# When the weights of a second MoE are prepared and where its input is staged: hooks replaced by slots of their own, three more staging places

## The chip, the cores and the metric

The kernel runs on one core of a Trainium2 chip. The time is device microseconds of one execution. TensorE (PE in the profile) does the matmuls, VectorE (DVE), ScalarE (ACT) and GpSimd (POOL) the elementwise work, and SyncE (SP) issues most of the DMAs. Each engine works through its own instructions in the order in which the program emits them and waits on semaphores for the others.

## The reference, cut to what matters

An attention with softmaxes over q and k gives x (2304 tokens x 512). A first mixture of experts (four experts of 1024 hidden columns, weighted by probabilities) is followed by a second layer, which the kernel calls the second MoE and which the change is about:

```
h = x @ w_in                       # 2304 x 512 @ 512 x 2048
g = where(h > 0, h, exp(min(h, 0)) - 1)
out = g @ w_out                    # 2304 x 2048 @ 2048 x 512
```

Everything is float32. A matmul is made of three in a faster format: each operand is split into a high part (a copy, on ACT) and a low part (the difference, on DVE or POOL), and the kernel adds high x high, high x low and low x high.

## The kernel before, in words

After the attention and the first expert, the work goes in 30 **steps** (s, b): s counts sets of four blocks of 128 hidden columns (s = 0 to 5 belong to the first MoE, s = 6 to 9 to the second), b = 0, 1, 2 counts thirds of the tokens. Step number i is 3 s + b, so the second MoE is steps 18 to 29. A step has 14 **products** (index `idx` 0 to 13: seven products of a Strassen-like scheme, for two halves `fp` of the hidden columns), each of six matmuls of 384 columns at line L1169. Between the products, PE does the second layer of the step before: six chunks of 12 matmuls (`chunk`, after s = 5), eight groups (`group`, after s = 6), or seven `turned_product`s after products 1, 2, 4, 6, 8, 11 and 13 (steps after s = 7, 8 and 9). The turned products take the weight parts in the order B11, T1, T2, B22, T3, B21, T4; the parts of set s are first used in the step after (s, 0), and each turned product reads the high part first and the low part in its second matmul.

After each product the loop emits the work of the other engines, in this order: the elementwise work of the product (`elu`: three ACT operations per quarter; its DVE part `rest` one or two products later; `flush` puts out the split of the results, an ACT copy at L1191 and a POOL difference at L1192), `drain`, the delayed additions of turned products (DVE, L1307), the DMA loads of the next step's input (`ring_load`, SP), the filling second-layer work, and then `tick`, which calls **hooks** up to a goal given in a table (`EARLY`, `PLAIN`, `MIXED`, `TURNED_HOOKS`); there are 24 hooks a step. Work for later steps is tied to hook numbers by `at2`.

Three kinds of such work matter here:

- `w1_steps(s, p)` prepares four weight tiles for half p of set s: four high parts `hi(0..3)` on ACT, low parts `lo(0..3)` on DVE or POOL, and two pairs of sums in place (`sums1`, `sums2`).
- `w2_fast` prepares the seven second-layer parts: `w2_sum` (DVE, L814) makes T1, T3, T2 and T4 in place; `w2_parts` makes the high part on ACT (L805) and the low part on POOL (L806).
- `turn_steps(b, c)` stages the input of the second MoE. For each third b of the tokens and each column c = 0, 1, 2, two accumulator tiles are transposed on PE (L957), copied back by ACT (L958), and seven pieces are formed with POOL differences (L992), copied to a place (`emit`, ACT or POOL), their low parts formed at L986, and stored to DRAM (L981). A place can be written again when its store has landed. There are six places, of which four are names that stand for tiles of their own (`y`, `qh`, `ql`, `extra`); in the second MoE other tiles replace these. `ring_load` reads the stored pieces back as the input of steps 18 to 20.

The transposes of column c need the accumulations of chunks c and c + 3 of the step before (DVE, L1258, after the chunks at idx 1, 3, 5, 8, 10 and 12). In the kernel before, column 2's begin at hook 22 of the same step, after product 13.

`w_load` reads raw weights from DRAM into two buffers that the two layers share, on SP's queue for s over 6. `CONV` times the conversion of float64 weights on DVE, which uses the tile `gt`; `gt` has four slots of 384 columns.

Of the kernel before, what the change touches and what calls it, by code (L numbers as in the profile page):

```python
# [21 lines left out]
def tile_attention_moe_moe(  # L22
# [13 lines left out]
    nc = tc.nc  # L36
# [676 lines left out]
    w1r, w2r, w1s, w2s = {}, {}, {}, {}  # L713

# [23 lines left out]
    def w1_steps(s, p):  # L738

        r, t = [], []  # L740

        def begin():
            r.append(w1r.pop((s, p)).rearrange("p j (d f) -> p j d f", d=KD))
            for _ in range(4):
                t.append(wp.tile([P, 2, KD, P], F32R, tag="w1", name="w1s"))
            if s % 2:
                t[0], t[2] = t[2], t[0]
            hi(0)

# [13 lines left out]

        tt = nc.vector.tensor_tensor

        def lo(k):
            eng = nc.gpsimd if k == 3 else nc.vector
            eng.tensor_tensor(out=dst(k, 1), in0=src(k), in1=dst(k, 0).bitcast(F32), op=ALU.subtract)

        def sums1():  # L770
            f1, f2 = r[0][:, 0], r[0][:, 1]
            tt = (nc.gpsimd if s == S_MOE else nc.vector).tensor_tensor
            tt(out=f1[:, :2], in0=f1[:, :2], in1=f2[:, :2], op=ALU.subtract)
            tt(out=f2[:, :2], in0=f2[:, :2], in1=f2[:, 2:], op=ALU.add)

        def sums2():
            f1, f2 = r[0][:, 0], r[0][:, 1]
            tt = (nc.vector if s > S_MOE and p else nc.gpsimd).tensor_tensor
            tt(out=f2[:, 2:], in0=f2[:, 2:], in1=f1[:, :2], op=ALU.subtract)
            tt(out=f1[:, 2:], in0=f1[:, 2:], in1=f2[:, 2:], op=ALU.subtract)  # L780

        if s > S_MOE:
            at_ = (-2, 0, 1, 4, 6, 6.5, 8, 9, 10, 11) if p else (-6, -4, -3, 1, 3, 4, 6, 8, 9, 11)
            return dict(zip(at_, (
                begin, lambda: lo(0), sums1, lambda: hi(1), lambda: lo(1), sums2,
                lambda: hi(2), lambda: lo(2), lambda: hi(3), lambda: lo(3),
            )))
# [12 lines left out]

    def w2_parts(s, op):

        src = w2_raw(s, W2_HOME.get(op, op))
        t = wp.tile([P, 2, 2, HALF_M], F32R, tag="w2", name="w2g")
        nc.scalar.activation(out=t[:, 0], in_=src, func=AF.Copy)  # L805
        nc.gpsimd.tensor_tensor(out=t[:, 1], in0=src, in1=t[:, 0].bitcast(F32), op=ALU.subtract)  # L806
        w2g[s, op] = t
# [8 lines left out]
    def w2_fast(i, s, d):  # L816

        for k, fn, op in (
            (8, w2_parts, "B11"), (14, w2_parts, "B22"), (16, w2_sum, "T1"), (17, w2_sum, "T3"), (18, w2_parts, "T1"),
            (20, w2_sum, "T2"), (21, w2_parts, "B21"), (24, w2_parts, "T2"), (30, w2_sum, "T4"), (31, w2_parts, "T3"),  # L820
            (35, w2_parts, "T4"),
        ) if s > S_MOE else (
# [5 lines left out]
            put(k - d, lambda fn=fn, op=op: fn(s, op))  # L828

# [46 lines left out]
    CONV += [(later, end1 + t, 1, True) for t in (11, 25, 39)]  # L876
# [7 lines left out]
    for i, (s, b) in enumerate(STEPS):  # L884
# [7 lines left out]
        if b == 0:  # L892

            a2, b2, c2, d2, a1, b1 = (2, 13, 25, 29, 34, 38)
            if s > 0 and (s <= S_FAST or SEVEN[s]):
                at2(i, 2, lambda s=s: w_load(s, 0, 1))
                at2(i, 13, lambda s=s: w_load(s, 1, 1))
                if SEVEN[s]:
# [7 lines left out]
            elif s > S_MOE:  # L906
                a1, b1 = (35, 40)
# [13 lines left out]
    stage = ["y", "qh", "ql", "extra", "ek"]  # L921

    def staged():
# [7 lines left out]
        if "ek" in stage:  # L931
            stage[-1:] = two(tmp, "ek")
        if now >= 0 and any(isinstance(t, str) for t in stage):
            stage[:] = two(stg, "r") + [t for t in stage if not isinstance(t, str)]
        if now >= 9 and len(stage) == 4:
# [478 lines left out]
    EARLY = {1: 4, 2: 8, 5: 12, 8: 16, 9: 20, 12: 22, 13: 24}  # L1414
    PLAIN, MIXED = ({1: 4, 3: 8, 5: 12, 8: 16, 10: 20, 12: 22, 13: 24}, {
# [13 lines left out]
    for i, (s, b) in enumerate(STEPS):  # L1429
# [11 lines left out]
        for fp in range(2):  # L1441
# [3 lines left out]
            for p in range(len(PRODUCTS)):  # L1445
# [52 lines left out]
                if i >= NB * S_MOE:  # L1498
                    drain()
# [23 lines left out]
    assert not timed2, sorted(timed2)  # L1523

# [49 lines left out]
```

## Time and profile before

| what | us |
|---|---|
| median of 3 runs | 1227.62 |
| lowest and highest | 1227.27 and 1228.93 |
| the profiled execution, its own time | 1229.85 |
| its span, first to last instruction | 1228.0 |

The profile is of one execution. It lists busy time by engine, what each engine waited for, and the clock that the throttle granted TensorE (1.00 is the full 2.4 GHz, 0.50 is 1.2 GHz). A wait for several semaphores is put down to the one that came last. An engine that is idle without being the one that others wait for costs nothing.

### The profile page before, as it was taken

What the parts mean: (1) busy time and instruction counts of PE and PEld (TensorE: products, weight loads), DVE (VectorE), ACT (ScalarE), POOL (GpSimd) and SP (SyncE); (2) the same over time, 40 slices, a digit from 0 to 9 for tenths busy, and PEclk for the clock granted to TensorE, in tenths of its full rate; (3) what the DMA queues carried; (4) which work ended last, traced back from release to release, by engine and by line L of the source; (5) the groups of instructions that cost most, each with busy time, mean ns of one, the idle gap of its engine ahead of it and who ended that gap; (6) DMA issues with size and microseconds to landing.
All of it is one profiled execution on the core that took longest, in us unless ns stands there. A gap on an engine that the chain in (4) does not pass through costs nothing.

```text
span 1228.0 us, 21080 instructions
## 1 busy us (share of the span) xinstructions
PE 1182.3 (96%) x7516; PEld 1126.5 (92%) x7516; DVE 913.1 (74%) x1523; ACT 674.7 (55%) x1431; POOL 640.2 (52%) x603
## 2 busy tenths in 40 slices
PE   8799999999999999999999999899999998898898
PEld 6688888889999999999999998788999998898898
DVE  6877887655787887787877876556557889889875
ACT  6544444236455455455455544446677776676663
POOL 4522543027468467467466453256336756756654
PEclk9999999999999999999999999889999999999999
DMA  9345666745767767667767677897965565365352
GB/s 257 113 128 161 205 217 222 265 173 215 250 226 254 261 228 250 258 234 254 254 240 253 249 244 280 283 305 257 318 245 196 195 221 181 124 228 170 148 205 103
DMA packets 157399, 272.34 MB, mean 222 GB/s; under 512 B 12784, under 2 KB 83952, under 8 KB 157296
## 3 DMA queue, kind: packets, MB, share of 16 engines
q1 hardware_dynamic: 155568, 267.87, 63.5%
q10 hardware_dynamic: 1728, 3.15, 0.7%
q8 instruction: 59, 0.97, 0.3%
q14 instruction: 44, 0.36, 0.1%
HBM read 224.83 MB, written 46.14 MB: 221 GB/s over the span
## 4 chain that ended last, share of the span: by engine, by line
PE 74%; DVE 12%; ACT 5%; DMA 4%; issue 3%; POOL 2%; SPq 0%; DVEq 0%; POOLq 0%; ACTq 0%
PE o L1387 18%; PE m L1169 14%; PE h L1169 14%; PE h L1028 7%; PE o L1028 7%; PE o L1298 6%; DVE accs L1307 2%; DMA xs<-staged 2%; DVE half L1218 1%; DMA xs<-stage 1%; PE o L1252 1%; PE o L1253 1%; PE o L1251 1%; DVE half L1219 1%; PE o L1273 1%
## 5 line engine op out<-in xcount | busy, mean ns | idle before, releaser
L1169 PE MATMUL m<-xh,w1s 128*128 128x384 f32 x840 | 250.0, 342 | 3.7 <-DVE half L1219 2.5
L1169 PE MATMUL h<-xh,w1s 128*128 128x384 f32 x840 | 246.0, 338 | 4.4 <-DVE m L1458 2.4
L1169 PEld LDWEIGHTS m<-xh,w1s 128*128 128x128 f32 x840 | 157.1, 191 | 9.6 <-DVE half L1219 4.0
L1169 PEld LDWEIGHTS h<-xh,w1s 128*128 128x128 f32 x840 | 155.7, 189 | 7.8 <-DVE m L1458 3.0
L1169 PE MATMUL m<-xl,w1s 128*128 128x384 f32 x420 | 142.5, 339 | 0.0
L1169 PE MATMUL h<-xl,w1s 128*128 128x384 f32 x420 | 141.3, 336 | 0.0
L1028 PE MATMUL o<-w2t,hpa 128*128 128x512 f32 x432 | 118.2, 401 | 0.8 <-DVE hpa L1060 0.5
L1028 PE MATMUL h<-xh,w1t 128*128 128x256 f32 (+1 forms) x512 | 113.0, 299 | 0.1
L1028 PEld LDWEIGHTS h<-xh,w1t 128*128 128x128 f32 x512 | 86.8, 193 | 5.2 <-POOL w1t L442 0.3
L1387 PE MATMUL o<-w2g,xh 128*128 128x256 f32 x540 | 90.4, 282 | 0.0
L1028 PEld LDWEIGHTS o<-w2t,hpa 128*128 128x128 f32 x432 | 75.7, 189 | 14.9 <-DVE hpa L1060 2.4
L1387 PE MATMUL o<-w2g,hpa 128*128 128x256 f32 x540 | 89.0, 282 | 0.0
L1387 PE MATMUL o<-w2g,xl 128*128 128x256 f32 x540 | 87.3, 282 | 0.0
L1409 DVE SCALAR_TENSOR_TENSOR accs<-o,pn,accs 128x256 f32<-128x256 f32 x180 | 75.7, 475 | 14.8 <-PE o L1387 14.2
L806 POOL TENSOR_TENSOR w2g<-r,w2g 128x512 fp32r<-128x512 f32 x56 | 77.9, 1398 | 15.5 <-ACT w2g L805 15.1
L1169 PEld LDWEIGHTS m<-xl,w1s 128*128 128x128 f32 x420 | 80.3, 191 | 0.5
L1169 PEld LDWEIGHTS h<-xl,w1s 128*128 128x128 f32 x420 | 79.8, 190 | 0.4
L1387 PEld LDWEIGHTS o<-w2g,xh 128*128 128x128 f32 x540 | 78.1, 190 | 0.0
L1028 PE MATMUL h<-xl,w1t 128*128 128x256 f32 (+1 forms) x256 | 77.7, 304 | 0.0
L1387 PEld LDWEIGHTS o<-w2g,hpa 128*128 128x128 f32 x540 | 76.1, 190 | 0.2
L1387 PEld LDWEIGHTS o<-w2g,xl 128*128 128x128 f32 x540 | 75.7, 190 | 0.2
L1307 DVE TENSOR_TENSOR accs<-o,accs 128x768 f32<-128x768 f32 (+1 forms) x64 | 59.5, 935 | 12.2 <-PE o L1298 12.2
(309 smaller groups left out, 3011.1 us busy)
## 6 DMA issues: line engine op xcount, KB each, us to landing
xh<-xs SPq DMA_DIRECT2D x210, 384.0 KB, 5.6
xl<-xs SPq DMA_DIRECT2D x210, 384.0 KB, 6.2
r<-in_w_dram SPq DMA_DIRECT2D x56, 256.0 KB, 4.5
xs<-stage SPq DMA_DIRECT2D x38, 256.0 KB, 5.1
xs<-xh SPq DMA_DIRECT2D x21, 384.0 KB, 3.8
xs<-xl SPq DMA_DIRECT2D x21, 384.0 KB, 4.1
r<-scratch SPq DMA_DIRECT2D x24, 256.0 KB, 3.4
x<-in_w_in_dram SPq DMA_DIRECT2D x10, 512.0 KB, 3.9
```

The costliest lines, as they stand in the source:

```text
L806: nc.gpsimd.tensor_tensor(out=t[:, 1], in0=src, in1=t[:, 0].bitcast(F32), op=ALU.subtract)
L1028: nc.tensor.matmul(out, lhsT, rhs, **kw)
L1169: nc.tensor.matmul(dst, t[:, wl, c + dl, :], x[xl_][:, dl, :], start=(n == 0 and p < 2), stop=(n == 5), skip_group_check=True,)
L1218: nc.vector.scalar_tensor_tensor(out=m, in0=m, scalar=1.0, in1=t, op0=ALU.add, op1=ALU.mult)
L1219: nc.vector.scalar_tensor_tensor(out=g, in0=h, scalar=0.0, in1=m, op0=ALU.max, op1=ALU.add)
L1251: nc.tensor.matmul(o, gh, w[:, 0, :], start=(f == 0), stop=False)
L1252: nc.tensor.matmul(o, gh, w[:, 1, :], start=False, stop=False)
L1253: nc.tensor.matmul(o, gl, w[:, 0, :], start=False, stop=(f == FS - 1))
L1298: nc.tensor.matmul(y[:, m], l, r, start=(n == 0 and k in STARTS), stop=(n == 5), skip_group_check=True)
L1307: nc.vector.tensor_tensor(out=a, in0=y[:, ms], in1=a, op=ALU.add)
L1387: nc.tensor.matmul(o, l, r, start=(first_write and m == 0 and c != 1), stop=(m == 5), skip_group_check=True)
L1409: nc.vector.scalar_tensor_tensor(out=a, in0=sums[x][:, c * HALF_M : (c + 1) * HALF_M], scalar=pr, in1=a, op0=ALU.mult, op1=ALU.add)
```

## The change

- **Staging.** Column 0 of a third starts at hook 7 (with one empty turn ahead), column 1 at hook 23 (product 13), column 2 at hook 3 of the next step. All columns go through `streams`, one entry per product and at most two streams at a time; before, only the last third did, and only from step 18. Three more places in `gt` join the list from step 17 on. Two conversions on `gt` move 3 and 6 hooks earlier, and `PLAIN` and `EARLY` reach hook 24 at product 12.
- **Slots.** For s = 7, 8 and 9 each operation of `w1_steps` and of the second-layer preparation is put at a product of its own (`put_at`; index -12 to 26, counted from product 0 of step (s, 0)) and is emitted after that product's own work and `drain`. High and low parts are emitted apart.
- **Engines.** For each of these sets, five operations go from POOL to DVE: the second pair of sums of half 0, `lo(3)` of half 0, and the low parts of T2 and B21.
- **Roles.** The four tiles of a half change roles from set to set, so that each is written when the set before has read it last.
- **Raw loads.** The next set's are tied to hooks 38 and 46, before 35 and 40.

```diff
-            eng = nc.gpsimd if k == 3 else nc.vector
+            eng = nc.gpsimd if k == 3 and (p or s <= S_MOE) else nc.vector
...
-            tt = (nc.vector if s > S_MOE and p else nc.gpsimd).tensor_tensor
+            tt = (nc.vector if s > S_MOE else nc.gpsimd).tensor_tensor
...
         if s > S_MOE:
-            at_ = (-2, 0, 1, 4, 6, 6.5, 8, 9, 10, 11) if p else (-6, -4, -3, 1, 3, 4, 6, 8, 9, 11)
-            return dict(zip(at_, (
+            i = NB * s
+            for idx, fn in zip((-5, -4, 1, -3, 2, 2, 3, 4, 4, 5) if p else (-12, -11, -11, -10, -9, -5, -4, -2, -2, 0), (
                 begin, lambda: lo(0), sums1, lambda: hi(1), lambda: lo(1), sums2,
                 lambda: hi(2), lambda: lo(2), lambda: hi(3), lambda: lo(3),
-            )))
+            )):
+                put_at(i, idx, fn)
+            return {}
...
+    def w2_slots(i, s):
+
+        for idx, fn, *a in (
+            (5, w2_hi, "B11"), (6, w2_lo, "B11"), (10, w2_sum, "T1"), (11, w2_hi, "T1"), (11, w2_sum, "T3"),
+            (12, w2_lo, "T1"), (12, w2_hi, "B22"), (13, w2_lo, "B22"), (15, w2_sum, "T2"), (16, w2_hi, "T2"),
+            (17, w2_lo, "T2", nc.vector), (18, w2_hi, "T3"), (19, w2_lo, "T3"), (23, w2_hi, "B21"),
+            (24, w2_lo, "B21", nc.vector), (24, w2_sum, "T4"), (25, w2_hi, "T4"), (26, w2_lo, "T4"),
+        ):
+            put_at(i, idx, lambda fn=fn, a=a: fn(s, *a))
...
+        if now >= -SH and not more_places:
+            y = gt.rearrange("p k n -> p (k n)").bitcast(F32R)
+            more_places.extend(y[:, k * DM : (k + 1) * DM].rearrange("p (l n) -> p l n", l=2) for k in range(3))
+            stage[:0] = more_places
...
-        for c, n0 in enumerate((8, 16, 22)):
-            fns = turn_steps(b, c)
-            if b == NB - 1:
-                at2(i, n0 - (n0 == 22), lambda f=fns: streams.append([lambda: (f[0](), f[1]()), *f[2:]]))
-                continue
-            for m, n in enumerate((0, 1, 2, 4, 5, 7, 8)):
-                if i * SH + n0 + n >= NB * S_MOE * SH:
-                    at2(i, 23, lambda f=fns[m:]: streams.append(f))
-                    break
-                at2(i, n0 + n, fns[m])
+        for c, n in enumerate((7, SH - 1, SH + 3)):
+            f = turn_steps(b, c)
+            f[:2] = [lambda f=(f[0], f[1]): (f[0](), f[1]())]
+            at2(i, n, lambda f=[lambda: None] * (c == 0) + f: streams.append(f))
...
-                if i >= NB * S_MOE:
-                    drain()
+                drain()
+                for fn in slots.pop((i, idx), ()):
+                    fn()
```

The old list of `w2_fast` for s over 6 had both parts of B11, B22, T1, B21, T2, T3 and T4 at hooks 8, 14, 18, 21, 24, 31 and 35 (the last is product 6 of step (s, 1)), and the sums T1, T3, T2 and T4 at hooks 16, 17, 20 and 30.

## Rows read from the trace of the kernel before

**Rows 1.** The page: busy time of PE, and its granted clock by slices.
```profile
PE 1182.3 (96%) x7516; PEld 1126.5 (92%) x7516; DVE 913.1 (74%) x1523; ACT 674.7 (55%) x1431; POOL 640.2 (52%) x603
PEclk9999999999999999999999999889999999999999
```
**Rows 2.** Windows, steps 16-19, 22, 24-26: length, PE, PEld, DVE, ACT, POOL, PEclk, DMA.
```profile
736.82:776.67 39.85, 34.88 (x182) 31.18 (x181) 23.52 (x40) 15.59 (x31) 12.03 (x12) 0.94 0.86 301
776.67:815.49 38.82, 35.93 (x183) 32.36 (x181) 20.59 (x34) 17.57 (x36) 15.85 (x19) 0.94 0.91 295
815.49:853.78 38.29, 36.12 (x183) 32.66 (x181) 21.84 (x34) 23.50 (x51) 19.72 (x23) 0.94 0.72 237
853.78:888.59 34.81, 33.43 (x184) 32.79 (x183) 17.34 (x29) 22.57 (x49) 16.66 (x19) 0.95 0.98 322
...
951.11:980.98 29.87, 29.63 (x170) 29.08 (x169) 26.24 (x38) 23.44 (x50) 22.00 (x20) 1.00 0.52 190
...
1010.11:1044.84 34.73, 30.89 (x170) 28.95 (x169) 33.22 (x45) 21.78 (x47) 21.72 (x19) 1.00 0.56 195
1044.84:1079.91 35.07, 31.32 (x169) 30.68 (x169) 28.27 (x40) 24.09 (x51) 22.98 (x20) 0.95 0.43 158
1079.91:1109.06 29.15, 29.15 (x170) 29.14 (x169) 24.65 (x39) 21.08 (x46) 16.35 (x17) 1.00 0.60 214
```
**Rows 3.** Waits of PE from 700 us on: total, times, longest.
```profile
PE o L957 <- DVE accs L1258: 10.0, 3, 5.0
PE o L1298 <- DVE accs L1307: 9.5, 6, 2.8
```
**Rows 4.** Timeline of PE, around 775, 853 and 1054 us.
```profile
775.08 1.30 PE L957 MATMUL o<-ident,accs 128*128 128x128 f32 x5 [4.97 <-DVE accs L1258]
...
852.93 1.09 PE L957 MATMUL o<-ident,accs 128*128 128x128 f32 x8 [2.17 <-DVE accs L1258]
...
1054.25 3.31 PE L1298 MATMUL o<-hpa,w2g 128*128 128x384 f32 x12 [2.79 <-DVE accs L1307]
```
**Rows 5.** Waits of DVE from 700 us on.
```profile
DVE stage L986 <- DMA xs<-stage: 11.0, 4, 4.3
...
DVE staged L986 <- DMA xs<-staged: 7.8, 3, 3.1
```
**Rows 6.** Timeline of DVE at the end of step 16.
```profile
773.58 0.69 DVE L986 TENSOR_TENSOR stage<-accs,stage 128x512 fp32r<-128x512 f32 x1 [3.73 <-DMA xs<-stage]
774.19 0.74 DVE L1258 SCALAR_TENSOR_TENSOR accs<-o,pn,accs 128x512 f32<-128x512 f32 x1
```
**Rows 7.** DVE's groups by line and shape in steps 24 and 25.
```profile
L1218 DVE SCALAR_TENSOR_TENSOR half<-half 128x384 f32<-128x384 f32 x8 | 8.0, 999 | 1.3 <-ACT half L1209 1.2
...
L773 DVE TENSOR_TENSOR r<-r 128x256 f32<-128x256 f32 x1 | 1.1, 1120 | 0.0
```
**Rows 8.** The same view in step 26.
```profile
L773 DVE TENSOR_TENSOR r<-r 128x256 f32<-128x256 f32 x1 | 0.4, 418 | 0.0
```
**Rows 9.** POOL's groups by line and shape in steps 24 and 25.
```profile
L806 POOL TENSOR_TENSOR w2g<-r,w2g 128x512 fp32r<-128x512 f32 x7 | 10.3, 1465 | 1.2 <-ACT w2g L805 1.2
```
**Rows 10.** Timeline of PE, ACT, POOL, DVE, products 11 to 13 of step 25.
```profile
1073.87 0.57 DVE L1469 TENSOR_TENSOR h<-h,extra 128x384 f32<-128x384 f32 x1 [0.62 <-PE h L1169]
...
1076.99 0.49 ACT L1207 ACTIVATE extra<-m 128x384 f32<-128x384 f32 x1 [0.49 <-PE m L1169]
...
1077.83 2.24 PE L1298 MATMUL o<-xh,w2g 128*128 128x384 f32 x12
...
1078.50 0.51 ACT L1191 ACTIVATE hpa<-gt 128x384 fp32r<-128x384 f32 x1
...
1079.09 1.02 POOL L1192 TENSOR_TENSOR hpa<-gt,hpa 128x384 fp32r<-128x384 f32 x1 [1.50 <-ACT hpa L1191]
```
**Rows 11.** Windows right after two of the waits of Rows 4: granted clock.
```profile
775.08:778.90 3.82, 3.82 (x15) 3.82 (x16) 1.94 (x4) 2.12 (x4) 0.00 (x0) 0.50 0.99 333
```
**Rows 12.** Timeline of SP: the first input load of step 19.
```profile
838.70 0.60 SPq L710 DMA_DIRECT2D xh<-xs  x1
```

More of the change, by code (lines that the diff above doesn't have):

```diff
@@ L713, in tile_attention_moe_moe, with put_at @@
     w1r, w2r, w1s, w2s = {}, {}, {}, {}
+    slots, roles = {}, {}
+    def put_at(i, idx, fn):
+        slots.setdefault((i + idx // 14, idx % 14), []).append(fn)
     def w_load(s, p, layer):
@@ L745, in begin @@
                 t.append(wp.tile([P, 2, KD, P], F32R, tag="w1", name="w1s"))
-            if s % 2:
+            if s > S_MOE:
+                u = roles.get(p, list(range(4)))
+                roles[p] = [u[2], u[0], u[3], u[1]]
+                t[:] = [t[k] for k in roles[p]]
+            elif s % 2:
                 t[0], t[2] = t[2], t[0]
@@ L799, in tile_attention_moe_moe, with w2_hi, w2_lo @@
     W2_HOME = {"T1": "B11", "T3": "B12", "T2": "B22", "T4": "B21"}
-    def w2_parts(s, op):
[L803 to L807, printed above, removed]
+    def w2_hi(s, op):
+        t = wp.tile([P, 2, 2, HALF_M], F32R, tag="w2", name="w2g")
+        nc.scalar.activation(out=t[:, 0], in_=w2_raw(s, W2_HOME.get(op, op)), func=AF.Copy)
+        w2g[s, op] = t
+    def w2_lo(s, op, eng=None):
+        t = w2g[s, op]
+        (eng or nc.gpsimd).tensor_tensor(
+            out=t[:, 1], in0=w2_raw(s, W2_HOME.get(op, op)), in1=t[:, 0].bitcast(F32), op=ALU.subtract
+        )
+    def w2_parts(s, op):
+        w2_hi(s, op)
+        w2_lo(s, op)
     def w2_sum(s, op):
@@ L818, in w2_fast @@
         for k, fn, op in (
[L819 to L822, printed above, removed]
             (8, w2_parts, "B11"), (13, w2_sum, "T1"), (17, w2_parts, "T1"), (18, w2_parts, "B22"), (19, w2_sum, "T3"),
@@ L875, in tile_attention_moe_moe @@
     ]
-    CONV += [(later, end1 + t, 1, True) for t in (11, 25, 39)]
+    CONV += [(later, end1 + t, 1, True) for t in (11, 22, 33)]
     end2 = NB * S_MOE * SH
@@ L897, in tile_attention_moe_moe @@
                 at2(i, 13, lambda s=s: w_load(s, 1, 1))
-                if SEVEN[s]:
+                if s > S_MOE:
+                    w2_slots(i, s)
+                elif SEVEN[s]:
                     w2_fast(i, s, 0)
@@ L906, in tile_attention_moe_moe @@
             elif s > S_MOE:
-                a1, b1 = (35, 40)
+                a1, b1 = (38, 46)
             if more and not SEVEN[s] and not SEVEN[s + 1]:
@@ L918, in tile_attention_moe_moe @@
                 at2(i, 13 + n, fn)
-    stage = ["y", "qh", "ql", "extra", "ek"]
+    stage, more_places = ["y", "qh", "ql", "extra", "ek"], []
     def staged():
@@ L932, in staged @@
             stage[-1:] = two(tmp, "ek")
+        if now >= -SH and not more_places:
+            y = gt.rearrange("p k n -> p (k n)").bitcast(F32R)
+            more_places.extend(y[:, k * DM : (k + 1) * DM].rearrange("p (l n) -> p l n", l=2) for k in range(3))
+            stage[:0] = more_places
         if now >= 0 and any(isinstance(t, str) for t in stage):
             stage[:] = two(stg, "r") + [t for t in stage if not isinstance(t, str)]
-        if now >= 9 and len(stage) == 4:
+        if now >= 9 and len(stage) == 7:
             stage[:0] = two(stg, "r")
@@ L1413, in tile_attention_moe_moe @@
     CHUNKS = (3, 0, 4, 1, 5, 2)
-    EARLY = {1: 4, 2: 8, 5: 12, 8: 16, 9: 20, 12: 22, 13: 24}
-    PLAIN, MIXED = ({1: 4, 3: 8, 5: 12, 8: 16, 10: 20, 12: 22, 13: 24}, {
+    EARLY = {1: 4, 2: 8, 5: 12, 8: 16, 9: 20, 12: 24}
+    PLAIN, MIXED = ({1: 4, 3: 8, 5: 12, 8: 16, 10: 20, 12: 24}, {
         0: 2, 1: 4, 2: 6, 3: 7, 4: 9, 5: 10, 6: 13, 7: 14, 8: 16, 9: 17, 10: 19, 11: 20, 12: 23, 13: 24,
@@ L1523, in tile_attention_moe_moe @@
     assert not timed2, sorted(timed2)
+    assert not slots and not streams, (sorted(slots), streams)
 _OUTS = [((512, 2304), "float32")]
```

## The prediction

> **What bounds the kernel now.** The page comes first: PE is busy 96% of the span, so what is to be had is only where PE is idle or slow, and the clock line shows where to look: two slices fall below 9 [rows 1]. The windows by step show the rest. Step 26 is what a second-MoE step costs undisturbed: 29.15 us, no PE idle, clock 1.00. Steps 24 and 25 have the same matmuls and take 34.73 and 35.07; together they lose 69.80 - 58.30 = 11.5 us. The set s = 9 repeats this in steps 27 and 28, so these two sets lose 23.0. Step 22, the same place in set s = 7, loses 29.87 - 29.15 = 0.7 [rows 2].
>
> The other loss is in steps 16 to 19, while the input is staged. PE idles 4.97, 2.89, 2.17 and 1.38 us there (length less PE's column), 11.4 in all. The clock's column, 0.94, 0.94, 0.94, 0.95, costs (1 - clock) x length, 2.4 + 2.3 + 2.3 + 1.7 = 8.7, of which I put 1.5 on idle time (an estimate). The loss is 11.4 + 7.2 = 18.6 us [rows 2]. Together with 23.0 and 0.7, 42.3 us are the most that could come back.
>
> What ends these waits: the two largest rows are transposes that wait for an accumulation on DVE (three times, up to 5.0), and turned products that wait for DVE's additions (six times) [rows 3]. The timeline gives single gaps; a low clock follows the large ones [rows 4], as after the first of them: 3.82 us at 0.50, the lower level of 1.2 GHz [rows 11].
>
> **Staging.** Why is DVE late at the end of step 16? Its accumulation at 774.19 stands right behind a low part that had waited 3.73 us for a store to free its place [rows 6]; such waits recur [rows 5]. Column 2's transposes follow one product after the chunk whose accumulation they need. The change moves them to product 2 of the next step: products 0, 1, 2 and one chunk later. Twelve matmuls of 384 columns take 2.08 us (from 1077.83 to the step's end at 1079.91 [rows 2, 10]), so a product takes 1.04 and a chunk, 12 of 512 columns, 2.8: 3 x 1.04 + 2.8 = 5.9 us. That is more than any of the three waits (4.97 at most), and with nine places instead of six, and stores begun before the input loads crowd the same queue, DVE should be less late as well. I take the three waits and the clock behind them as gone.
>
> Against that, two streams at once now run in products 2 to 4 of steps 17 to 19, with ACT, DVE and POOL work of two columns in one product. Step 19, which already had such an overlap before, idled 1.38 with no transposes late. I leave 1 us of new wait in each of three steps: 3.0. Bounds: 1 (only step 19's remains) and 10 (half of today's). Gain 18.6 - 3.0 = **15.6**, between 8.6 and 17.6. The moved transposes and conversions are the same instructions and cost nothing; their cover is the slack of engines that are 30 to 65% busy there [rows 2].
>
> **Weight work on DVE.** In step 24 DVE is busy 33.22 of 34.73 us, in step 26 24.65 of 29.15 [rows 2]. Part of that is lost in collisions with POOL: the same 256-column sum takes 1.120 us in step 24 and 0.418 in step 26, and the 384-column step L1218 has a mean of 0.999 [rows 7, 8]. The five operations that move are per set: two sums (0.42 each on DVE without collision), and three 512-column low parts, by L773's 0.418 for half the columns 0.7 to 0.84 each; say 0.8 + 3 x 0.7 = 2.9 us more for DVE per set. For POOL they are three of L806's 1.465 and two sums of about half, 5.9 us less [rows 9].
>
> By step, DVE without weights has about 24.65 - 2.6 = 22.0 in step 26 (two low parts, one half low part and two sums are its weights). After the change step b = 0 has 4.8 us of weight work (six low parts and sums of half 0 and 1, and the sums T1 and T3), b = 1 2.7, b = 2 4.1. That gives 26.8, 24.7 and 26.1 of 29.15, before further collisions. With POOL's weight work in b = 0 falling from six low parts to four, I add 2 us to b = 0: 28.8, nearly full. So I expect DVE to keep up, with 0.5 us of PE waits left in b = 0 and 0.5 for parts that are now made one product ahead. Bounds: 0 and today's 5.6 (step 24's loss).
>
> **A new wait: the low part of T4.** This part goes from product 6 to product 12 of step b = 1, and the turned product that reads it follows product 13. The order of emission decides: after product 12 come ACT's three operations for that product's quarter, the ACT copy and POOL difference of the quarter before (flush), and only then the slot with T4's low part, on POOL. In step 25, an undisturbed stretch, product 12 has ended by 1076.79 (the turned product's start at 1077.83 less product 13's 1.04), ACT begins the quarter at 1076.99, the copy runs at 1078.50, POOL's difference at 1079.09 until 1080.11; PE starts the turned product at 1077.83, and its second matmul would be 0.17 later (2.08 us / 12), at 1078.00 [rows 10]. T4's low part can start at 1080.11 and takes 1.465 [rows 9]: it ends at 1081.6. PE waits 3.6 us. Two more operations on DVE (low part of B21, sum of T4) now stand in front of L1469 at 1073.87 [rows 10], and by 0.7 to 1.7 us the ACT chain behind it shifts. I take 1.0: **4.6 us**, bounds 3.4 and 5.4. A wait of that length lies between those of 2.17 and 4.97, both followed by a low clock: 3.82 us at half speed cost 1.9 [rows 4, 11]. I add 2.0 (bounds 0 and 3). So 6.6 us in each of steps 22, 25 and 28. The Trainium skill (TensorE: Matmul & The Clock Gate, section "Architectural detail") states that ACT and DVE are strictly first in, first out, and GpSimd too for each of its cores; by that rule POOL cannot take T4's part ahead of the waiting difference, and rows 10 agree: POOL is idle for 1.50 us before it.
>
> What is queued behind it on POOL: the differences of the next quarters, which wait for ACT anyway until after the step's end; SP's raw load for the next set at hook 46 waits for this part too, with no input load behind it until product 7 of the next step.
>
> T1's low part has the same place in step 24, but is read after product 2 of step 25, two fills and four products later; T3's falls at product 5 and is read after product 8, with 0.5 us to spare. Both cost nothing beyond the 0.5 above.
>
> **Roles and raw loads** take away waits of ACT for tiles still being read; no wait of PE is laid to them, and I put them at nothing. Their cover is that tiles free two products before they are rewritten; without it the cost is one product, 1.0 us per set.
>
> **The sum.** Sets 8 and 9: today 11.5 each, after 6.6 + 1.0 = 7.6: gain 3.9 x 2 = 7.8. Set 7: today 0.7, after 6.6 + 0.5 = 7.1: loss 6.4. Staging: gain 15.6. Net gain 15.6 + 7.8 - 6.4 = 17.0. The profiled execution of 1229.85 (span 1228.0) goes to 1212.9; the median, 2.2 lower, 1227.6 to **1210.6**.
>
> **Rivals.**
> *The wait for T4 is not paid.* PE could reach this turned product late anyway, because DVE still holds it up, or the order on POOL could leave more room than I read. Then the three 6.6 fall away: 1210.6 - 19.8 = 1191, or 1195 with 1 us each left and the clock intact. Against it: step 25's stretch from product 9 on runs undisturbed [rows 2, 10]. Chance 0.2.
>
> *DVE stays the bound.* The collisions follow POOL's busy time, 21.7 and 23.0 us in steps 24 and 25 [rows 2]; taking 5.9 of 44.7 away leaves 87% of them. Then step 24's 5.6 stays and T4's 6.6 is added: 12.2 against 11.5, a loss of 0.7 x 2, and with 6.4 for set 7 the time is 1227.6 - 15.6 + 1.4 + 6.4 = 1220. The Trainium skill (SBUF — State Buffer, section "Who interferes with whom") has a rule for it: a VectorE instruction with two SBUF inputs and a GpSimd instruction that reads SBUF exclude each other for a whole instruction. L773 with 1.120 against 0.418 agrees [rows 7, 8]. Against it: step 26, with 16.35 of POOL, has little of it [rows 2]. Chance 0.13.
>
> *More places don't help.* DMA was busy 0.86 to 0.98 in steps 16, 17 and 19 [rows 2]; if the engines and not the places delay the stores, DVE waits as before and half the gain goes, 7.8 us: 1218. Chance 0.1.
>
> *Slower: the input lands late.* The last store of a column falls at product 7 instead of about 4, some three products and two chunks (8.7 us) later, at the very loads that read it back. The first load of step 19 was issued at 838.70, 15.1 us before the step began at 853.78 [rows 2, 12]. With 5 us to land and the waits of 2 to 4 us gone from the step's end, 6 us are left. If each load waits 12 us more for its store, steps 18, 19 and 20 wait 6 us each and lose 2 to the clock: 24, against the 17 of the forecast: 1210.6 + 24 = 1235. It decides from 5.5 us late per step. Against it: of the column's seven pieces only the last two are so late. Chance 0.07.
>
> **How the numbers follow.** The forecast has 0.5; its own range, from the bounds of the T4 wait (three times 3.4 to 8.4) and of staging, not all taken at one end, is 1203 to 1219. The range of 1195 to 1222 takes in the first rival's upper half, DVE and the places. About 0.2% is what a measurement of this kernel tells from no change: under 1225.2 faster. Faster 0.5 + 0.2 + 0.1 + most of 0.13 = 0.90; same 0.04; slower 0.06.
>
> **What would show it.** Right: no transposes among PE's waits; one gap of 3 to 5 us before the last turned product of steps 22, 25, 28, ended by POOL's low part, with a low clock after it; step 24 near 30 us and step 25 near 36; step 22 longer than before. Wrong: PE waiting for DVE's additions as before, DMA among PE's waits in steps 18 to 20, or step 22 undisturbed.

## The result: 0.8% slower, and the profile after

| | us |
|---|---|
| before, median of 4 runs (range) | 1228.28 (1227.27 to 1230.26) |
| after, median of 4 runs (range) | 1237.97 (1236.81 to 1238.73) |
| ratio, 95% interval | 1.0076, 1.0059 to 1.0094 |
| forecast | 1210.6, range 1195 to 1222 |

The kernel became slower, and the time lies outside the range. From the page of after, PE's busy time and its clock by slices; they answer to [rows 1]:

```profile
PE 1182.8 (96%) x7516; PEld 1126.6 (91%) x7516; DVE 924.3 (75%) x1537; ACT 673.0 (54%) x1430; POOL 627.0 (51%) x590
PEclk8999999999999999999999999999999899899989
```

The two 8s of before are gone; one stands in the first slice now and three near the end. The lines of the program have moved: in after, L1194 are the products, L1323 the turned products, L1332 their additions on DVE, L1217 POOL's differences of the quarters, L776 and L820 the low parts of the first and second layer's weights. In a timeline the bracket gives the idle time before a row and what ended it. The windows of after for steps 16 to 19, 22 and 24 to 26 (columns as in [rows 2]), and a stretch inside step 25:

```profile
735.69:768.97 33.28, 33.21 (x173) 29.75 (x173) 20.16 (x37) 12.77 (x26) 8.36 (x8) 1.00 0.76 267
768.97:802.95 33.98, 33.98 (x183) 30.80 (x182) 21.43 (x36) 17.26 (x37) 15.95 (x19) 1.00 1.06 354
802.95:840.03 37.08, 34.47 (x184) 30.64 (x182) 22.32 (x37) 23.39 (x50) 22.23 (x27) 1.00 0.84 275
840.03:873.25 33.22, 32.49 (x191) 32.14 (x190) 18.23 (x29) 24.59 (x53) 17.39 (x21) 1.00 0.92 314
936.81:974.50 37.69, 32.39 (x169) 30.60 (x169) 33.48 (x45) 23.66 (x50) 22.91 (x19) 0.94 0.54 189
1004.80:1040.01 35.21, 30.26 (x170) 29.02 (x170) 33.33 (x48) 23.39 (x51) 19.48 (x17) 1.00 0.57 201
1040.01:1080.51 40.50, 33.45 (x169) 32.23 (x169) 34.16 (x46) 23.56 (x50) 22.83 (x19) 0.90 0.50 176
1080.51:1110.74 30.23, 30.23 (x169) 30.22 (x169) 22.70 (x34) 19.96 (x43) 14.33 (x13) 0.96 0.43 145
...
1076.00:1082.80 6.80, 5.97 (x19) 5.98 (x20) 4.20 (x6) 0.13 (x1) 0.77 (x1) 0.50 0.66 216
```

Against [rows 2], steps 16 to 19 are 14.2 us shorter and run at full clock (step 20 gives 1.0 back). Step 22 is 7.8 longer, step 24 0.5 longer although POOL works 2.2 less in it, step 25 5.4 longer. DVE is busy 90.2 us in steps 24 to 26, before 86.1.

What PE waited for from 700 us on in after (total, times, longest), which answers to [rows 3]:

```profile
PE o L1323 <- POOL w2g L820: 12.2, 3, 4.1
PE o L1323 <- DVE accs L1332: 8.5, 6, 2.3
PE m L1194 <- DVE half L1244: 3.3, 2, 1.7
PE h L1194 <- DVE m L1483: 3.2, 2, 1.6
PE h L1194 <- ACT m L1479: 2.7, 2, 2.0
```

The transposes' row of 10.0 us is gone. In its place stands one with 12.2: the turned products that wait for T4's low part on POOL. The row of DVE's additions has hardly changed (8.5 for 9.5, six times in both), and two more rows of DVE stand under it. The single gaps in the timeline of PE, steps 24 and 25 of after, beside [rows 4]:

```profile
1007.66 0.44 PE L1194 MATMUL m<-xh,w1s 128*128 128x384 f32 x1 [1.66 <-DVE half L1244]
...
1013.79 0.81 PE L1323 MATMUL o<-hpa,w2g 128*128 128x384 f32 x3 [1.67 <-DVE accs L1332]
...
1032.59 0.44 PE L1194 MATMUL h<-xh,w1s 128*128 128x384 f32 x1 [1.62 <-DVE m L1483]
...
1047.63 2.73 PE L1323 MATMUL o<-hpa,w2g 128*128 128x384 f32 x10 [2.26 <-DVE accs L1332]
...
1076.83 1.65 PE L1323 MATMUL o<-xh,w2g 128*128 128x384 f32 x4 [4.07 <-POOL w2g L820]
```

The gap at 1076.83 is the forecast one. The clock is 0.50 for 6.8 us there (the window above), from 0.83 us before PE goes on to 5.97 after. The four before it are DVE's. The timeline of DVE and POOL in step 24 shows what makes DVE late:

```profile
1024.85 0.64 DVE L1248 TENSOR_TENSOR gt<-half,gt 128x384 f32<-128x384 f32 x1
1025.04 1.60 POOL L776 TENSOR_TENSOR w1s<-r,w1s 128x512 fp32r<-128x512 f32 x1
1025.53 1.53 DVE L1249 TENSOR_TENSOR gt<-gt 128x384 f32<-128x384 f32 x1
1026.59 1.61 POOL L820 TENSOR_TENSOR w2g<-r,w2g 128x512 fp32r<-128x512 f32 x1
1026.97 1.64 DVE L1250 TENSOR_TENSOR half<-half,gt 128x384 f32<-128x384 f32 x1
1028.16 1.32 POOL L1217 TENSOR_TENSOR hpa<-gt,hpa 128x384 fp32r<-128x384 f32 x1
1028.54 1.36 DVE L1243 SCALAR_TENSOR_TENSOR half<-half 128x384 f32<-128x384 f32 x1
```

Two low parts and a quarter's difference follow each other on POOL, and three 384-column operations of DVE take 1.53, 1.64 and 1.36 us, where 0.56 is their time with POOL out of the way (shown below). Each of the three ends 0.41 or 0.42 us after the POOL operation beside it has ended (for L1249: 1027.06 against 1026.64), as if it had to let that one pass first. The slots of their own put the two low parts beside DVE's own work.

### The profile page after: what moved, and what is told of

Read it like the earlier page. It is cut to its first block, busy times and chain, and to the rows that moved or that the text cites. A ratio compares the mean times of both kernels' runs of the same rounds, so it can differ in the third digit from the quotient of the medians.

```text
span 1236.9 us, 21090 instructions
## 1 busy us (share of the span) xinstructions
PE 1182.8 (96%) x7516; PEld 1126.6 (91%) x7516; DVE 924.3 (75%) x1537; ACT 673.0 (54%) x1430; POOL 627.0 (51%) x590
## 4 chain that ended last, share of the span: by engine, by line
PE 68%; DVE 12%; issue 6%; POOL 6%; ACT 5%; DMA 3%; SPq 0%; DVEq 0%; POOLq 0%; ACTq 0%
PE o L1412 18%; PE m L1194 13%; PE h L1194 12%; PE h L1053 7%; PE o L1053 6%; PE o L1323 3%; DMA xl<-xs 2%; DVE accs L1332 2%; POOL w2g L820 2%; PE o L1277 1%; PE o L1278 1%; PE o L1276 1%; POOL xl L1217 1%; DVE half L1244 1%; ACT half L1233 1%
## 5 line engine op out<-in xcount | busy, mean ns | idle before, releaser
L1194 PE MATMUL h<-xh,w1s 128*128 128x384 f32 x840 | 245.6, 338 | 7.3 <-DVE m L1483 3.2
L1194 PE MATMUL m<-xh,w1s 128*128 128x384 f32 x840 | 248.3, 340 | 3.9 <-DVE half L1244 3.3
L1194 PEld LDWEIGHTS h<-xh,w1s 128*128 128x128 f32 x840 | 155.6, 189 | 10.4 <-DVE m L1483 3.9
L1194 PEld LDWEIGHTS m<-xh,w1s 128*128 128x128 f32 x840 | 156.4, 190 | 8.7 <-DVE half L1244 3.9
L1194 PE MATMUL m<-xl,w1s 128*128 128x384 f32 x420 | 141.9, 338 | 0.0
L1194 PE MATMUL h<-xl,w1s 128*128 128x384 f32 x420 | 141.1, 336 | 0.0
L1053 PEld LDWEIGHTS h<-xh,w1t 128*128 128x128 f32 x512 | 86.1, 192 | 5.2 <-POOL w1t L442 0.3
L1053 PEld LDWEIGHTS o<-w2t,hpa 128*128 128x128 f32 x432 | 75.6, 189 | 14.9 <-DVE hpa L1085 2.4
L1194 PEld LDWEIGHTS m<-xl,w1s 128*128 128x128 f32 x420 | 80.2, 191 | 0.5
L1194 PEld LDWEIGHTS h<-xl,w1s 128*128 128x128 f32 x420 | 79.7, 190 | 0.3
L820 POOL TENSOR_TENSOR w2g<-r,w2g 128x512 fp32r<-128x512 f32 x50 | 71.6, 1444 | 11.0 <-ACT w2g L814 11.0
L1217 POOL TENSOR_TENSOR hpa<-gt,hpa 128x384 fp32r<-128x384 f32 x27 | 29.4, 1094 | 80.9 <-ACT hpa L1216 66.8
```

The lines of the kernel that those rows point to most:

```text
L820: (eng or nc.gpsimd).tensor_tensor(out=t[:, 1], in0=w2_raw(s, W2_HOME.get(op, op)), in1=t[:, 0].bitcast(F32), op=ALU.subtract)
L1053: nc.tensor.matmul(out, lhsT, rhs, **kw)
L1194: nc.tensor.matmul(dst, t[:, wl, c + dl, :], x[xl_][:, dl, :], start=(n == 0 and p < 2), stop=(n == 5), skip_group_check=True,)
L1217: nc.gpsimd.tensor_tensor(out=gl, in0=g, in1=gh.bitcast(F32), op=ALU.subtract)
```

## The experiments

Each time below is the median of four executions (no roles: five), and each ratio is against the kernel before, run beside it. These medians of before lie between 1225.79 and 1227.63 us, so kernels of different rounds are compared by ratio.

### Staging alone, weight work alone

*Only staging*: the weight preparation of before, the staging of after. *Only slots*: the other half.

> The staging part alone, with the weights prepared as before. Theory (the loss lies in the weight slots): steps 16 to 20 as in the changed kernel, which took 13.2 us less there than before, and steps 22, 24, 25, 27, 28 as before: 1228 - 13 = 1215. Rival (the staging part gives its gain back later, in the second MoE's own steps): above 1222.

> The slots, engines, roles and raw loads alone, with the staging as before. Theory: the sets s = 7, 8, 9 lose what they lose in the changed kernel, 9.0 + 7.0 + 6.9 = 22.9 us more than before: 1251. Rival (the two parts disturb each other): under 1243.

Measured: staging alone 1219.24 us, ratio 0.9928 (0.9909 to 0.9946); slots alone 1246.87, ratio 1.0158 (1.0143 to 1.0173). The two are worth -8.4 and +19.2 us against 1227.63 beside them; their sum, +10.9, is close to the whole change's +9.7. Each lies between its theory's and its rival's time, 4 us from the theory's. That staging alone has 8.4 where steps 16 to 20 of after are 13.2 shorter lies, in its profiled execution, in two steps: step 18 is 1.6 longer than in after (the last section shows why), and step 20 3.0 longer, with a wait of 2.08 us for DVE and a low clock of 3.4 us at it. In slots alone PE waits for the transposes as before ("L984" is the transposes' line there):

```profile
PE o L1325 <- POOL w2g L820: 12.2, 3, 4.1
PE o L984 <- DVE accs L1285: 9.7, 3, 5.2
```

So the staging takes those waits away by itself, and the weight work costs more than twice what the staging brings.

### T4's low part early

```diff
-            (17, w2_lo, "T2", nc.vector), (18, w2_hi, "T3"), (19, w2_lo, "T3"), (23, w2_hi, "B21"),
-            (24, w2_lo, "B21", nc.vector), (24, w2_sum, "T4"), (25, w2_hi, "T4"), (26, w2_lo, "T4"),
+            (17, w2_lo, "T2", nc.vector), (18, w2_hi, "T3"), (19, w2_lo, "T3"), (19, w2_hi, "B21"),
+            (20, w2_lo, "B21", nc.vector), (20, w2_sum, "T4"), (21, w2_hi, "T4"), (22, w2_lo, "T4"),
```

> The changed kernel with B21's parts at slots 19 and 20, T4's sum at 20, its high part at 21 and its low part at 22, not 23 to 26. Theory (T4's low part is queued on POOL behind a difference that waits for ACT): the three gaps of 4.07 us and the low clock behind them, 6.83 us at half speed, go: 3 x (4.2 + 3.0) = 21.6 off, 1216. Rival (DVE holds PE up there anyway, and the wait only changes its name): another wait of 2 us or more at the same turned product, and above 1230.

Measured: 1219.76 us, ratio 0.9932 (0.9917 to 0.9946). The edit moves five operations, B21's two parts, T4's sum and T4's two parts, four products forward; that is worth 18.2 us, some 6.1 for each of three steps. The three gaps are gone, as the theory said; its 1216 is missed by 4 us, because other waits show in their place. Steps 24 and 25 of this kernel, and PE's waits:

```profile
998.92:1034.14 35.22, 30.27 (x169) 29.01 (x169) 33.33 (x48) 23.38 (x51) 19.48 (x17) 1.00 0.57 202
1034.14:1068.45 34.31, 31.28 (x169) 30.64 (x169) 29.45 (x39) 23.10 (x49) 22.25 (x19) 0.95 0.46 165
```

```profile
PE o L1323 <- DVE accs L1332: 9.3, 9, 2.3
PE h L1194 <- ACT m L1479: 5.3, 5, 2.0
PE m L1194 <- DVE half L1244: 3.3, 2, 1.7
```

POOL is no longer among these waits, but steps 24 and 25 take 35.22 and 34.31, about what they took before (34.73 and 35.07). With the staging's gain kept, the weight slots alone are at best even. What remains is DVE, and the next runs take it apart.

### Which DVE work, and in which order

*Slots after adds*: in after, a product's slots are emitted behind the delayed additions of the turned products, not ahead of them. *W1 back*: in the kernel with T4 early, the second sums and the fourth low part of half 0 go back to POOL. *No roles*: the same kernel with the old exchange of tiles. The edits:

```diff
-                for fn in slots.pop((i, idx), ()):
-                    fn()
                 if idx != 7:
                     flush_adds()
+                for fn in slots.pop((i, idx), ()):
+                    fn()
```
```diff
-            eng = nc.gpsimd if k == 3 and (p or s <= S_MOE) else nc.vector
+            eng = nc.gpsimd if k == 3 else nc.vector
...
-            tt = (nc.vector if s > S_MOE else nc.gpsimd).tensor_tensor
+            tt = (nc.vector if s > S_MOE and p else nc.gpsimd).tensor_tensor
```
```diff
-            if s > S_MOE:
-                u = roles.get(p, list(range(4)))
-                roles[p] = [u[2], u[0], u[3], u[1]]
-                t[:] = [t[k] for k in roles[p]]
-            elif s % 2:
+            if s % 2:
```

> The changed kernel with the slots emitted after the delayed additions and not ahead of them. Theory A (a weight operation on DVE stands ahead of the addition that PE waits for): the waits on L1332's like, 1.67 and 2.26 us in each of sets 8 and 9, shrink by about 1 us each, and with the low clock after the second 1234 to 1236 are left. Theory B (DVE is late through collisions with POOL, and the order of one operation changes nothing): 1237 to 1239, or slower, since T4's and B21's parts get later still.

> t4_early with the second pair of sums and the fourth low part of half 0 back on POOL, as before the change. Theory A (collisions): DVE has 1.5 us less of its own and POOL 3.2 us more at the same places; each POOL operation there costs DVE up to 1 us, so it comes out even: 1218 to 1222. Theory B (own load): step 24 falls by 1.5 us in each of two sets, 1215 to 1217.

> The kernel of t4_early without the tiles' change of roles (tiles 0 and 2 change places in every second set, as before). Theory A (roles take away only waits of ACT that nothing on the way to the end stands behind, as the prediction says): t4_early's time, 1218 to 1222 us. Theory B (ACT's high parts now wait for tiles still being read, and DVE and PE behind them): 1224 us or more, with ACT's high parts waiting for PE.

Measured: slots after adds 1237.91, ratio 1.0085 (1.0068 to 1.0102), as after itself; w1 back 1219.47, ratio 0.9941 (0.9924 to 0.9958), as T4 early; no roles 1220.02, ratio 0.9946 (0.9925 to 0.9967), as T4 early. With the additions ahead of the slots, the waits of 1.66 and 1.67 at the first products of step 24 shrank to 0.16 and 0.24, but that of 1.62 grew to 2.21: the wait changed its place. Step 24 itself fell from 35.21 to 33.78. Three operations more or less on DVE make no difference either. The change of roles is worth nothing that can be measured, as forecast.

### Is it what POOL reads, or how long POOL works?

All three kernels here are T4 early with one thing more, and each leaves out part of the computation. *No sums* leaves out the sums of the weights of both layers in sets 7 to 9. *POOL memset* replaces POOL's weight low parts in these sets by one memset each, of the same tile; *POOL memset 3* by three memsets in a row, so that POOL is occupied as long as before.

```diff
+            if k == 3 and p and s > S_MOE:
+                for _ in range(3):
+                    nc.gpsimd.memset(dst(k, 1).bitcast(F32), 0.0)
+                return
...
+        if eng is None and s > S_MOE:
+            for _ in range(3):
+                nc.gpsimd.memset(t[:, 1].bitcast(F32), 0.0)
+            return
```

> t4_early with the in-place sums of the weights left out for s = 7, 8, 9 (eight short ones and four long ones a set, some 6 us of DVE), so that parts are made of the raw weights; POOL's work stays. Theory A (collisions): each long DVE operation that meets a POOL low part still takes 1 us more, the waits of step 24 and of step 25's first products shrink only in part: 1210 to 1216. Theory B (own load): steps 24 and 25 fall to 30 us or less, 1200 to 1207.

> t4_early with POOL's six weight low parts of a set (five of the second layer and one of the first) replaced by a POOL memset of the same tile: the subtraction is left out, so these parts are zero. POOL writes as much and reads nothing. Theory A (in steps 24 and 25 DVE is late through collisions with POOL's reads): DVE's busy time of 35.4 us in step 24 falls to 29 to 31, PE's waits of 1.67, 1.68, 1.61 and 2.29 us shrink to 2 us together, steps 24 and 25 take 30 to 31.5 us, and the time falls from 1219.8 to 1203 to 1208. Theory B (DVE has too much work of its own there): DVE stays over 33 us, and the time stays above 1214.

> The kernel of pool_memset with each low part on POOL written as three memsets in a row (some 3 x 0.525 = 1.6 us of POOL, as long as the subtraction took beside DVE, but reading nothing from SBUF); the low parts' values are left out of the computation. Theory A (DVE is slowed by what POOL's subtraction reads): the time stays with pool_memset, 1200 to 1206 us, steps 25 and 28 at 29 to 30 us. Theory B (the subtraction's length on POOL's queue delays POOL's sums and the tiles that wait for them): back to t4_early's 1213 to 1222 us, steps 25 and 28 at 33 us or more.

Measured: no sums 1207.92, ratio 0.9849 (0.9834 to 0.9864), between its two theories; POOL memset 1201.80, ratio 0.9798 (0.9783 to 0.9813), even below theory A's range; POOL memset 3 1200.63, ratio 0.9783 (0.9759 to 0.9808), in theory A's range. POOL memset missed in one place: step 24 took 33.34 us and not 30 to 31.5, and its first two waits stayed. (The 35.4 us that its expectation gives for DVE in step 24 are 33.33 in the window above.) POOL memset 3 is the test. DVE's groups by line and shape in steps 24 and 25, first of after, then of POOL memset 3, where these lines are L1251, L1257 and L1258:

```profile
L1249 DVE TENSOR_TENSOR gt<-gt 128x384 f32<-128x384 f32 x5 | 6.7, 1331 | 0.2
L1243 DVE SCALAR_TENSOR_TENSOR half<-half 128x384 f32<-128x384 f32 x9 | 6.6, 736 | 1.1 <-ACT half L1234 1.1
...
L1250 DVE TENSOR_TENSOR half<-half,gt 128x384 f32<-128x384 f32 x5 | 4.9, 987 | 0.0
```

```profile
L1251 DVE SCALAR_TENSOR_TENSOR half<-half 128x384 f32<-128x384 f32 x8 | 4.4, 554 | 0.6 <-ACT half L1242 0.6
...
L1257 DVE TENSOR_TENSOR gt<-gt 128x384 f32<-128x384 f32 x4 | 2.2, 558 | 0.1
L1258 DVE TENSOR_TENSOR half<-half,gt 128x384 f32<-128x384 f32 x4 | 2.2, 552 | 0.0
```

POOL's memsets in the same steps of that kernel (15 are 5 low parts), and its steps 24 to 26:

```profile
L826 POOL MEMSET w2g<- 128x512 f32 x15 | 7.8, 527 | 0.6
```

```profile
993.74:1027.05 33.31, 30.00 (x170) 29.06 (x170) 30.77 (x48) 23.14 (x50) 19.05 (x21) 1.00 0.53 188
1027.05:1056.25 29.20, 29.20 (x169) 29.11 (x169) 25.20 (x41) 23.09 (x49) 21.70 (x27) 1.00 0.57 205
1056.25:1085.38 29.13, 29.13 (x170) 29.12 (x169) 25.81 (x40) 20.52 (x45) 14.49 (x14) 1.00 0.62 220
```

The memsets still stand beside the same work of DVE, here in the timeline of POOL and DVE in step 24:

```profile
1013.94 1.70 POOL L778 MEMSET w1s<- 128x512 f32 x3
1014.45 0.56 DVE L1257 TENSOR_TENSOR gt<-gt 128x384 f32<-128x384 f32 x1
1014.93 0.55 DVE L1258 TENSOR_TENSOR half<-half,gt 128x384 f32<-128x384 f32 x1
```

POOL is busy there for 55.25 us over the three steps (the sum of its column), with T4 early 56.55: nearly the same. DVE, with the same instructions, falls from 89.75 to 81.78, and the time by 1.5 points of the ratio, some 18 us. The length of POOL's low parts is not what costs; that they read SBUF while DVE adds is. The Trainium skill (SBUF — State Buffer, section "Who interferes with whom") says just this: a VectorE instruction with two SBUF inputs contends with a GpSimd instruction that reads SBUF, and not with one that only writes it. The traces agree: the same operation takes 0.56 us beside memsets (L1257 here), and in after (L1249) 1.50 to 1.54 in the four of five cases with a low part beside it and 0.56 in the fifth, which is the mean of 1.33. L1332, which has one of its two inputs in PSUM, takes 0.94 to 0.96 in all 15 cases of after's steps 24 and 25, 12 of them beside POOL's differences.

That settles steps 25 and 28, which fall from 34.31 and 34.29 to 29.21. It doesn't settle step 24: of its 6.1 us over step 26 of before, 4.2 stay, with two waits of 1.65 and 1.66 at its first products. What POOL's low parts read has no share in these. In slots after adds, where the additions stand ahead of DVE's own low parts L776, the two were 0.16 and 0.24, so these waits hang on the order of DVE's work.

No sums, with POOL's low parts kept, brings some 10 us by the ratios (0.9932 to 0.9849). It doesn't separate DVE's own time from collisions: DVE's sum over steps 24 to 26 falls by 9.4, but four long sums of 0.68 and eight short ones of 0.42, their times without a POOL operation beside them, make only 6.1 a set.

### Other slots: three versions that beat both kernels

*Windows* starts from after and gives the parts other slots; *windows 2* and *windows 3* mend the largest wait that the one before had left. The slots of windows 3, with the slots emitted behind the additions:

```diff
-            for idx, fn in zip((-5, -4, 1, -3, 2, 2, 3, 4, 4, 5) if p else (-12, -11, -11, -10, -9, -5, -4, -2, -2, 0), (
-                begin, lambda: lo(0), sums1, lambda: hi(1), lambda: lo(1), sums2,
-                lambda: hi(2), lambda: lo(2), lambda: hi(3), lambda: lo(3),
+            for idx, fn in zip((-5, -3, -3, -3, 2, 2, 2, 2, 3, 3) if p else (-12, -10, -11, -11, -9, -9, -8, -7, -3, -4), (
+                begin, lambda: hi(1), lambda: lo(0), sums1, lambda: lo(1), sums2,
+                lambda: hi(2), lambda: hi(3), lambda: lo(3), lambda: lo(2),
...
+            (3, w2_hi, "B11"), (3, w2_lo, "B11"), (9, w2_sum, "T1"), (10, w2_hi, "T1"), (10, w2_lo, "T1"),
+            (10, w2_hi, "B22"), (11, w2_lo, "B22"), (15, w2_sum, "T3"), (15, w2_sum, "T2"), (16, w2_hi, "T3"),
+            (16, w2_hi, "T2"), (16, w2_hi, "B21"), (16, w2_lo, "T2", nc.vector), (16, w2_lo, "T3"), (16, w2_lo, "B21"),
+            (20, w2_sum, "T4"), (22, w2_hi, "T4"), (23, w2_lo, "T4"),
```

The raw loads of the second layer move up by two and three hooks as well, and B21's low part goes back to POOL.

> The changed kernel with the same engines' work placed anew: DVE's weight operations after products 2 to 6, where it had gaps in step 26, POOL's low parts after products 2, 3, 9, 10 and 11, where POOL has run out of the quarters' differences, none beside the run of two-input operations at the start of each half; slots after the additions; the low part of B21 on POOL. Theory A: steps 24 and 25 near 30 us, 1200 to 1208. Theory B (own load, whatever the place): 1214 or more.

> The kernel of windows with the half's operations begun ten products earlier in steps 24 and 27, the low parts of half 1 moved to products 2 to 3 of the next pass, and tile 1's sum and parts at products 9 and 10, so that DVE's half L1243 no longer stands before the 3.1 us wait of products 7 to 8. Theory A (the wait is a matter of position): the 3.1 us of each set go, steps 24 and 27 near 31 us, and the time is 1203 to 1209 us. Theory B (DVE has no spare time in these stretches): the wait comes back at other products, 1210 us or more.

> The kernel of windows2 with half 0's slots put back to those of windows, and the low part of T2 one product earlier (16, ahead of the two low parts on POOL). What is left of waits in windows2 is 1.75 us in steps 23 and 26 at product 8 (0.52 in windows), and 1.0 to 1.5 us for T2's low part on DVE in steps 22, 25 and 28. Theory A (each wait belongs to one slot): 1.2 us go in each of steps 23 and 26 and 1.0 in each of three steps, some 5 to 6 with the clock: 1202 to 1207 us. Theory B (DVE is full and a wait only changes its place): 1208 us or more.

Measured: windows 1211.95 (ratio 0.9879, 0.9856 to 0.9902) and windows 2 1209.98 (0.9867, 0.9842 to 0.9893), both between their two theories and not to be told from each other; windows 3 1206.56 (0.9836, 0.9808 to 0.9863), in theory A's range. In windows 2 steps 24 and 27 did come down to 31.4 and 30.7, but steps 23 and 26 rose to 31.3 and 32.8 with waits for the same DVE line: there, a wait changed its place. Windows 3 took the better of both: 31.95 and 31.96 us in steps 24 and 27 (windows 34.09 and 33.91), 29.96 and 29.92 in steps 23 and 26 (windows 29.93 and 29.94). Its largest wait for DVE is now in step 20: 2.46 us, with a low clock at it, and the step takes 35.6 us where after's takes 32.4. Steps 24 and 25 of windows 3:

```profile
1001.07:1033.02 31.95, 29.70 (x170) 29.06 (x169) 29.21 (x43) 23.11 (x50) 21.23 (x19) 1.00 0.58 203
1033.02:1062.98 29.96, 29.72 (x169) 29.03 (x169) 27.67 (x42) 22.90 (x47) 21.24 (x18) 1.00 0.51 188
```

DVE's groups by line and shape in these steps; the lines are L1243, L1249 and L1250 of after:

```profile
L1242 DVE SCALAR_TENSOR_TENSOR extra<-extra,half 128x384 f32<-128x384 f32 x9 | 8.2, 908 | 0.7 <-ACT extra L1233 0.7
...
L1248 DVE TENSOR_TENSOR gt<-gt 128x384 f32<-128x384 f32 x4 | 2.2, 559 | 0.1
L1249 DVE TENSOR_TENSOR half<-half,gt 128x384 f32<-128x384 f32 x4 | 2.2, 552 | 0.0
```

POOL works for 42.5 us in the two steps, in the kernel before for 44.7. What has changed is which operations of DVE meet its low parts: of the last two lines none stands beside one, of the first five of nine (in after none; its mean is 0.908 us, in after 0.633). DVE's sum over steps 24 to 26 is 83.4 us, 6.8 less than in after. The three versions change the slots, the order of the additions, the raw loads and the engine of one low part together, so what the slots bring by themselves isn't shown.

## Why the prediction was wrong

Term by term, in us; the forecast's terms are those of its sum, the measured ones are differences of step lengths in the profiled executions of before, T4 early and after:

| term | forecast | measured |
|---|---|---|
| staging | -15.6 | -13.2 (steps 16 to 20) |
| T4's wait, three steps | +19.8 | +19.1 (after against T4 early, steps 22 to 29; by the medians 18.2) |
| DVE in sets 7, 8, 9, without T4 | -21.2 | +4.0 (T4 early against before, steps 22 to 29) |
| before step 16 | 0 | -1.1 (step 16 begins at 735.69 for 736.82) |
| sum | -17.0 | +8.9 (span 1228.0 to 1236.9; from unrounded terms) |

The forecast for DVE is the 0.7 + 11.5 + 11.5 lost before, less the 0.5 + 1.0 + 1.0 that was to stay. The measured +4.0 are +2.9 in steps 22 and 23, +0.7 in 24 to 26, +0.5 in 27 to 29. Step 16 began between 734.2 and 736.9 us in all these kernels, so the -1.1 is no effect of the change.

**Staging: right in its mechanism.** No transpose waits, no DMA among PE's waits, steps 16 to 19 at clock 1.00. For the 3.0 us of new waits that were allowed for, PE idled 37.08 - 34.47 = 2.61 in step 18 and 0.73 in step 19; step 20 took 1.0 more than before, which the forecast did not have. DVE's waits for the stores, the 11.0 and 7.8 us of [rows 5], have no row in after any more, and the two rivals about places and late input are out. The size differs: in the other eleven profiles with this staging, steps 16 to 20 are 8.4 to 13.3 us shorter than before, and by its median staging alone brought 8.4, just under the lower bound of 8.6. Which of its parts, the later columns, the streams or the places, brings the gain was not tried.

**T4: right, and near in size.** The wait is 4.06 or 4.07 in each of the three steps, forecast 4.6 with bounds 3.4 and 5.4. It ends as the forecast's chain said, here in the timeline of POOL of after:

```profile
1074.24 1.00 POOL L1217 TENSOR_TENSOR hpa<-gt,hpa 128x384 fp32r<-128x384 f32 x1 [1.41 <-ACT hpa L1216]
1075.20 1.57 POOL L820 TENSOR_TENSOR w2g<-r,w2g 128x512 fp32r<-128x512 f32 x1
```

The low clock lasts 6.8 us, 6.0 of them after the wait, and so costs 3.0, the upper bound, not 2.0. The 4.07 + 3.0 = 7.1 of the gap is more than the 6.1 that came back by the medians when it was taken away: in T4 early other waits show in its place (ACT's row there has 5.3 us in five waits, in after 2.7 in two).

**DVE: the failed step.** "So I expect DVE to keep up, with 0.5 us of PE waits left in b = 0 and 0.5 for parts that are now made one product ahead." Step 24 took 35.21 for the 29.65 that this makes, and step 25 still loses 5.2 us with T4 early. Of the prediction's own signs, these two steps failed ("step 24 near 30 us and step 25 near 36", measured 35.2 and 40.5), and one of its signs of being wrong came: PE waits for DVE's additions as before. The count of work was right: three low parts and two sums more, which without a POOL operation beside them take 0.68 and 0.42 us each, 2.9 together. But the step costed them "before further collisions", added 2 us for b = 0 alone, and took the collisions before to shrink with POOL's busy time. They did not: POOL's sum over steps 24 to 26 fell from 61.1 to 56.6, DVE's rose by 4.1, 1.2 more than the 2.9 of added work. A collision here is not a share of two engines' busy time; it is a meeting of one POOL instruction that reads SBUF with one instruction of DVE that has both inputs in SBUF (0.56 against 1.50 to 1.54 for the same line), and the slots decide which ones meet. The forecast gave DVE 28.8, 24.7 and 26.1 us in the three steps. T4 early has 33.33, 29.45 and 26.97; POOL memset 3, with the same work on DVE and without what POOL's low parts read, has 30.77, 25.20 and 25.81, close to the forecast.

The rival "DVE stays the bound" named the rule, with a chance of 0.13, but let only step 24's 5.6 stay and let step 25's loss go: hence its 1220. With step 25's 5.2 kept in each of sets 8 and 9, it would have said 1230.

So the missing 25.2 us of this term fall into two parts. In POOL memset 3, steps 22 to 29 are 18.9 us shorter than in T4 early: that much goes with what POOL's low parts read. They are then 14.9 shorter than before, not 21.2: the other 6.3 are steps 24 and 27, which keep 4.2 each, mostly the two waits at their first products, where the forecast left 1.0 for a whole set.

The forecast's range failed for the same reason: its bound "today's 5.6" was one step's loss, where both steps' stayed, in two sets.

**What stays open.** No version kept the low parts on POOL and was free of collisions, so how much of the 18 us can be had by placing alone isn't known; by the ratios, windows 3 is 12 us below T4 early. The two waits at the first products of step 24 stay in POOL memset 3. Putting the additions ahead took them away in slots after adds, but another wait grew and the time stayed; with the collisions gone, that order wasn't tried. A memset also doesn't wait for the high part, so it can start earlier than a subtraction; the memsets shown above stand beside the same operations of DVE, but what an earlier start may bring elsewhere wasn't separated.

## What to carry to other kernels

Before work goes from POOL to DVE, or to other places on POOL, list which DVE instructions with two inputs in SBUF will run beside which POOL instructions that read SBUF, and cost them at the collided duration (here 1.1 to 1.6 us for 0.4 to 0.6); the net count of work said little here. Where an operation gets a slot of its own, compare the slot with the first reader of its result, and with what stands ahead of it on its engine: four products were worth 18 us, in three places. And test a large change in its parts: one half of this one was a gain, and the other hid it.

## What the runs showed of the hardware

The same wait of 2.01 us in step 18 was followed by the low clock in one execution and not in another. In staging alone, PE's timeline and the window behind it:

```profile
829.51 0.45 PE L1190 MATMUL h<-xh,w1s 128*128 128x384 f32 x1 [2.01 <-ACT m L1475]
```

```profile
830.20:833.60 3.40, 3.40 (x10) 2.83 (x9) 1.51 (x2) 0.42 (x1) 3.24 (x6) 0.50 0.94 275
```

And in after:

```profile
828.33 0.45 PE L1194 MATMUL h<-xh,w1s 128*128 128x384 f32 x1 [2.01 <-ACT m L1479]
```

```profile
828.30:831.70 3.40, 3.37 (x16) 2.98 (x17) 1.36 (x3) 0.83 (x2) 3.24 (x5) 1.00 0.98 264
```

Step 18 takes 38.65 us in the one and 37.08 in the other. T4 early and no roles differ there in the same way, 37.07 and 38.59: in single executions, a step can be 1.5 us longer with the same waits in it. Of the twelve profiles with this staging, six have the low clock behind this wait and six don't. Somewhat longer waits were no surer: one of 2.24 us in windows 2 was followed by clock 1.00, one of 2.26 in after by 3.4 us at 0.50. At each of after's three waits of 4.06 or 4.07 the clock was 0.50 for 6.8 us, from 0.7 to 1.0 us before the wait's end; in slots alone and in slots after adds, one of three such waits had 3.4 us at 0.50 only.
